# Attention scores contracted over 128 rows instead of twice 64, with q transposed by DMA in later pairs

## The chip, the cores and the metric

The kernel runs on one core of a Trainium2 chip. The metric is device time in microseconds, from the start to the end of one execution. Engines are named as in the profile: PE (TensorE, matmuls; its weight loads are PEld), DVE (VectorE), ACT (ScalarE), POOL (GpSimd), SP (SyncE, which here only issues DMAs).

## The reference

Two stages, with batch 4, 8 heads, 768 positions, head size 64.

The first is attention that chooses chunks. Keys are cut into 24 chunks of 32. For each query and chunk an upper bound of the score is computed from the chunk's elementwise minimum and maximum; causally later chunks get −1e9; the six chunks with the highest bounds are kept:

```python
k_min = np.min(k_chunks, axis=3); k_max = np.max(k_chunks, axis=3)
ub = np.sum(np.maximum(q * k_min, q * k_max), axis=-1)      # per query and chunk
ub = np.where(causal, ub, -1e9)
top_chunks = np.argsort(ub, axis=-1)[..., -6:]
scores = np.where(sel & causal_by_position, scale * (q @ k.T), -1e9)
attn = softmax(scores); x = attn @ v
```

The second is a gated MLP on `x` (heads side by side, 512 wide): `h = relu(x @ w_in)` with 1024 columns, halves `u` and `v`; `v` is normalised over its 512 columns, multiplied from the left by the 768×768 matrix `w_spatial`, a bias is added; the output is `(u * v_s) @ w_out`, in float32.

## The kernel before

Everything is cut into operations that a planner in the kernel (class `Plan`, L80) puts into one fixed order per engine before the program is written. Each operation has a list of engines that can do it with a cost for each, a priority (a due time), and the tiles that it reads and writes. The planner always takes one of the operations that can start soonest (within 60 ns) and of these the one with the lowest priority value, on the engine where it would end first. Tiles come from rings of a fixed number of buffers (L298 to L334). So a change of costs, ring sizes or operations shifts the order everywhere. On the chip every engine runs its list in order: an instruction that waits holds everything behind it on its engine, and the same goes for SP's list of DMAs.

The attention is done for 16 pairs of heads (4 batches of 4 pairs). Per pair `i`:

- `load` (L414): k, q and v of both heads by SP's DMAs, 384 KB each (L422).
- `prep` (L425): k and q are cast to float16 on POOL (`n16`, through the helper `copy`, L287 to L291). q is transposed by PE in all pairs, k by PE in pairs 0 to 3 (L442, six 128×128 transposes into PSUM), evacuated to `qT` and `kT` by ACT or DVE. In pairs 4 to 15 k is transposed by a DMA through the crossbar (L450) straight into `kT`. In the transposed tiles rows 0 to 63 are head 0 and rows 64 to 127 head 1. From `kT` DVE takes the chunk maxima and minima (`kh_half` L468 halves the chunk, `kmm` L471 reduces; from PSUM in one step, L460, in pair 0), from `qT` the positive and the negative part (`rq`, L481). PE multiplies them to bounds `ub` (L489); DVE adds the causal mask (L496), takes the eight largest of each row (L502, L507), and writes to `sn` what is not selected and a guard (L510, L513). PE transposes `sn` (L522), ACT or DVE evacuates it to `selT` (L525).
- `attend` (L530): scores of both heads, masked by adding a second product: `expand`, a constant pattern that spreads 24 chunks to 768 columns with −30000, times `selT`. For each strip of a key tile by up to 512 queries there are four matmuls of 64 rows: head 0 and head 1 of k·q (L546), then head 0 and head 1 of pattern·selection (L549), which are added in PSUM. Rows 0 to 63 and 64 to 127 hold the two heads. Six groups of strips per pair fill PSUM tiles `sc` (two buffers of 128×1024). ACT takes the exponential (L556), POOL zeroes the upper triangles (L566), PE multiplies with v (`av`, L578; a column of ones gives the sum), DVE takes reciprocals (L581) and normalises into `x16` (L584). `x16` is transposed by PE in pairs 0 to 7 and 15 (L597), otherwise by the crossbar (L603).

`mlp` (L608) runs once per batch when its four pairs are done: projections of v and u (L621), relu (L628 on ACT, L630 on DVE), statistics (L639, L642), normalisation (L654, DVE), the spatial product (L669), gating (L673), a transpose of the gated tile (L683 on PE in batches 0 and 3, else crossbar L689), the output projection (L695), its evacuation and the store (L699). The planner fits this into the gaps of later pairs' attention; the last batch has no attention beside it. `w_spatial` is transposed on PE at the beginning (L407).

The costs that the planner used for PE's scores include an entry for a switch of the row mode, `SWITCH = 60.0` ns a group (L551); a DMA costs a length and a common 1900 ns until it has landed.

Of the kernel before, what the change touches and what calls it, by code (L numbers as in the profile page):

```python
# [14 lines left out]
P = 128  # L15
# [7 lines left out]
LAT = {"PE": 210.0, "DVE": 130.0, "ACT": 140.0, "POOL": 160.0, "DMA": 1900.0}  # L23
# [6 lines left out]
def t_act(n):  # L30
    return n / 1.2 + 70.0
# [33 lines left out]
class Op:  # L65
    def __init__(self, name, opts, fn, prio):
        self.name, self.opts, self.fn, self.prio = name, opts, fn, prio
        self.preds, self.succs, self.bufs = set(), [], []
        self.opens = []
        self.dma = 0.0  # L70
        self.lazy = False
        self.start = self.end = self.ready = None
        self.eng = None
# [6 lines left out]
class Plan:  # L80
# [11 lines left out]
    def op(self, name, opts, fn, prio, reads=(), writes=(), dma=0.0, after=None, lazy=False):  # L92
# [32 lines left out]
    def run(self, window=60.0):  # L125
# [11 lines left out]
        while avail:  # L137
# [35 lines left out]
            if o.dma:  # L173
                dma_free = max(dma_free, s + d) + o.dma
                o.end = dma_free + LAT["DMA"]
            else:
                o.end = s + d
# [27 lines left out]
    def report(self, total):  # L205
# [4 lines left out]
        print("DMA", round(sum(o.dma for o in self.done)))  # L210
# [3 lines left out]
XBAR = 1200.0  # L214
PE_T = {("q", i) for i in range(16)} | {("k", i) for i in range(4)}
SWITCH = 60.0
# [7 lines left out]
LOAD = 1750.0  # L224
BACKLOG = 4000.0

STRIPS = [
    [(0, 0, 512, 0)],  # L230
    [(1, 128, 512, 0)],
    [(2, 256, 512, 0)],
    [(3, 384, 256, 0), (5, 640, 128, 256), (3, 640, 128, 384)],
    [(0, 512, 256, 0), (4, 512, 256, 256)],
    [(1, 640, 128, 0)],
]
WIDTHS = [512, 512, 512, 512, 512, 128]
DIAG = [(0, 2), (0, 2), (0, 2), (0, 4), (256, 2), None]
BANK = 512
EW = 2 * sum(WIDTHS)  # L240


def block_column(t, qi):
    for g, strips in enumerate(STRIPS):
        for (tt, q0, n, col) in strips:
            if tt == t and q0 <= qi * P < q0 + n:
                return g, col + qi * P - q0
    raise KeyError((t, qi))
# [3 lines left out]
def kernel(  # L252
# [49 lines left out]
    ring("kT", 4, [P, NQT, P])  # L302
    ring("qT", 4, [P, NQT, P])
    ring("selT", 3, [P, S])
# [7 lines left out]
    ring("e", 3, [P, EW])  # L312
# [20 lines left out]
    ring("ex24", 1, [P, 2, NCH], F32)  # L333
    ring("expand", 1, [P, S])  # L334
# [23 lines left out]
    ex24, expand = buf("ex24"), buf("expand")  # L358

    def mk_ex(e):  # L360
        for hi in range(2):
            x = ex24.t[:, hi, :]
            e.memset(x, 0.0)
            e.affine_select(out=x, in_=x, compare_op=Alu.not_equal, fill=NEG,
                            base=-hi * D, channel_multiplier=1, pattern=[[-1, NCH]])
            e.affine_select(out=x, in_=x, compare_op=Alu.not_equal, fill=-1.0,
                            base=-(hi * D + NCH), channel_multiplier=1, pattern=[[0, NCH]])
    preset("ex24", {"POOL": 1400.0}, mk_ex, [ex24], prio=-60.0)
    for hi in range(2):
        r0, r1 = hi * D, (hi + 1) * D  # L370
        preset(f"expand{hi}", {"ACT": 720.0},
               lambda e, hi=hi, r0=r0, r1=r1: copy(
                   e, expand.t[r0:r1].rearrange("p (c j) -> p c j", j=CHUNK),
                   ex24.t[r0:r1, hi].unsqueeze(2).to_broadcast([r1 - r0, NCH, CHUNK])),
               [(expand, hi)], reads=[ex24], prio=-50.0)
# [6 lines left out]

    preset_pool("vt", 80.0, lambda e, t: e.memset(t[:, :, :, D:D + 2], 1.0), -80.0)
# [4 lines left out]
    CAST0 = {"DVE": t_dve(S, 2)}  # L388
# [4 lines left out]
    def weights():  # L393
        for n, dst, src, cost in (("w_in", w_in, moe_w_in.rearrange("(o p) f -> p o f", p=P), 6200.0),
# [3 lines left out]
               0.0, writes=[dst], dma=cost, after=W_AFTER[n], lazy=True)  # L398
        op("bcol", {"SP": 350.0}, lambda e: e.dma_start(out=bcol.t, in_=moe_b_spatial.rearrange("(t p) -> p t", p=P)),
           30.0, writes=[bcol], dma=1200.0)  # L400
# [24 lines left out]
    def prep(i, prio):  # L425
# [3 lines left out]
        for n in ("k", "q"):  # L429
            nat = buf("n16")  # L430
            tT = st[n + "T"] = buf(n + "T")
# [3 lines left out]
            op(f"c_{n}{i}", CAST0 if i == 0 else CAST, go, prio, reads=[st[n]], writes=[nat])  # L435
            if (n, i) in PE_T:
                tr = buf("gen")

                def go(e, nat=nat, tr=tr):
# [4 lines left out]
                op(f"e_{n}{i}", {"ACT": t_act(S)} if i == 0 else EVAC,  # L444
                   lambda e, tr=tr, tT=tT: copy(e, tT.t.rearrange("p t c -> p (t c)"), tr.t.bitcast(F16)[:, 0:S]),
                   prio + 0.05, reads=[tr], writes=[tT])
                src[n] = (tr, lambda tr=tr: tr.t.bitcast(F16)[:, 0:S])
            else:
                def go(e, nat=nat, tT=tT):
                    e.dma_start_transpose(out=tT.t, in_=nat.t.rearrange("p t h d -> p (t h d)"))  # L450
                op(f"x_{n}{i}", {"SP": 1250.0}, go, prio, reads=[nat], writes=[tT], dma=XBAR)
            if i > 0 or (n, i) not in PE_T:
                src[n] = (tT, lambda tT=tT: tT.t.rearrange("p t c -> p (t c)"))
        kb, kT = src["k"]
        qb, qT = src["q"]
        kmm, km = buf("kmm"), buf("km")
        if kb.pool.name == "gen":
            for m, f in ((0, Alu.max), (1, Alu.min)):
                op(f"kmm{m}_{i}", {"DVE": t_dve(S)},
                   lambda e, m=m, f=f: e.tensor_reduce(kmm.t[:, m, :], kT().rearrange("d (c j) -> d c j", j=CHUNK),  # L460
                                                       axis=AX.X, op=f),
                   prio, reads=[kb], writes=[(kmm, m)])
        else:
            hf = buf("kh_half")
            for m, f in ((0, Alu.max), (1, Alu.min)):
                def go(e, m=m, f=f):
                    x = kT().rearrange("d (c j) -> d c j", j=CHUNK)
                    e.tensor_tensor(hf.t[:, m], in0=x[:, :, 0:CHUNK // 2], in1=x[:, :, CHUNK // 2:CHUNK], op=f)  # L468
                op(f"kh{m}_{i}", {"DVE": t_dve(S // 2, 2)}, go, prio, reads=[kb], writes=[(hf, m)])
                op(f"kmm{m}_{i}", {"DVE": t_dve(S // 2)},  # L470
                   lambda e, m=m, f=f: e.tensor_reduce(kmm.t[:, m, :], hf.t[:, m], axis=AX.X, op=f),  # L471
                   prio, reads=[(hf, m)], writes=[(kmm, m)])
        for hi in range(2):
            r0, r1 = hi * D, (hi + 1) * D
            op(f"km{hi}_{i}", {"POOL": 250.0, "DVE": 100.0} if i else {"DVE": 100.0},
               lambda e, hi=hi, r0=r0, r1=r1: copy(e, km.t[r0:r1, :, hi, :], kmm.t[r0:r1]), prio,
               reads=[kmm], writes=[(km, hi)])
        rq = buf("rq")
        for m, f in ((0, Alu.max), (1, Alu.min)):
            op(f"rq{m}_{i}", {"DVE": t_dve(S, 2 if qb.pool.name == "gen" else 4)},  # L480
               lambda e, m=m, f=f: e.tensor_scalar(rq.t[:, m, :], in0=qT(), scalar1=0.0, scalar2=None, op0=f),  # L481
               prio, reads=[qb], writes=[(rq, m)])
# [41 lines left out]
        selT = st["selT"] = buf("selT")  # L524
        op(f"es{i}", EVAC, lambda e: copy(e, selT.t, tr.t.bitcast(F16)[:, 0:S]), prio, reads=[tr], writes=[selT])  # L525
# [4 lines left out]
    def attend(i, prio):  # L530
        b, hp = divmod(i, HP)
        st = pair.pop(i)
        kT, qT, selT, vt = st["kT"], st["qT"], st["selT"], st["vt"]
        x16, e_ = buf("x16"), buf("e")
        for g, strips in enumerate(STRIPS):
            sc = buf("sc")
            w = WIDTHS[g]

            def go(e, strips=strips, sc=sc):
                for (t, q0, n, col) in strips:  # L540
                    for half in range(2):
                        for hi in range(2):
                            r = slice(hi * D, (hi + 1) * D)
                            o = sc.t[:, hi * BANK + col:hi * BANK + col + n]
                            if half == 0:
                                e.matmul(o, lhsT=kT.t[r, t, :], rhs=qT.t[r].rearrange("p t c -> p (t c)")[:, q0:q0 + n],  # L546
                                         start=True, stop=False)
                            else:
                                e.matmul(o, lhsT=expand.t[r, t * P:(t + 1) * P], rhs=selT.t[r, q0:q0 + n],  # L549
                                         start=False, stop=True)  # L550
            op(f"sc{i}_{g}", {"PE": t_pe(*[2 * s[2] for s in strips]) + SWITCH}, go, prio,  # L551
               reads=[kT, qT, selT, expand], writes=[sc])

            def go(e, g=g, w=w, sc=sc):
                o = e_.t[:, 2 * BANK * g:2 * BANK * g + 2 * w].rearrange("p (h c) -> p h c", h=2)
                e.activation(out=o, in_=sc.t.rearrange("p (h c) -> p h c", h=2)[:, :, 0:w],  # L556
                             func=Act.Exp, scale=scale)
# [193 lines left out]
```

## Time and profile before

| | us |
|---|---|
| median of three runs | 229.11 |
| lowest, highest | 228.91, 230.06 |
| the profiled execution | 229.7 |
| its span, from the first to the last instruction | 228.0 |

| engine | busy us of the span | instructions |
|---|---|---|
| PE | 198.6 (87%) | 2226 |
| DVE | 171.9 (75%) | 564 |
| ACT | 136.2 (60%) | 195 |
| POOL | 81.1 (36%) | 157 |

The profile comes from one execution. A group of instructions is given by line, engine, operation and `out<-in` of the tiles, with count, busy time and mean length; the idle time of the engine just before the group and what ended it stand behind. PE's matmuls overlap, so a matmul's length is more than what it costs; the distance between the starts of two that follow each other without a gap is the cost. The same holds to a smaller degree on DVE and ACT. "Issue" of a DMA is SP's time; "landing" is when the data are there.

### The profile page before, as it was taken

How to read it: one execution, taken by the hardware profiler on the slowest of the kernel's cores; microseconds unless marked ns; L12 is line 12 of the kernel's file. 1: busy time of each engine (PE TensorE's matmuls, PEld its weight loads, DVE VectorE, ACT ScalarE, POOL GpSimd, SP SyncE). 2: the span in 40 equal slices, each digit the busy share in tenths (PEclk: the TensorE clock that was granted, in tenths of full speed). 3: DMA queues.
4: the chain of work that ended last, by engine and by line, in shares of the span. 5: the costliest groups of instructions: out<-in, count | busy, mean ns of one | idle time of the engine just before them, and what ended most of it. 6: DMA issues, size and time to landing. Idle time of an engine off the chain costs nothing.

```text
span 228.0 us, 5782 instructions
## 1 busy us (share of the span) xinstructions
PE 198.6 (87%) x2226; PEld 111.2 (49%) x2226; DVE 171.9 (75%) x564; ACT 136.2 (60%) x195; POOL 81.1 (36%) x157
## 2 busy tenths in 40 slices
PE   1167778879959699998999999999999999999982
PEld 0144546564625365656464646455535644444440
DVE  3686999686998899989987999969536955383430
ACT  5208577729726985639657793718688540775062
POOL 3226774343910674737363464322232100000000
PEclk9999999999979999999999999999999999999998
DMA  8999998999999769999999993223541004630024
GB/s 156 201 218 218 180 185 138 209 221 192 209 169 220 130 138 167 223 214 201 184 226 243 176 179 63 57 50 90 163 144 35 3 0 92 203 121 3 0 94 182
DMA packets 102331, 33.60 MB, mean 147 GB/s; under 512 B 97440, under 2 KB 98720, under 8 KB 102304
## 3 DMA queue, kind: packets, MB, share of 16 engines
q1 hardware_dynamic: 100464, 30.49, 71.9%
q0 software_dynamic: 1840, 2.75, 7.2%
q8 instruction: 17, 0.28, 0.5%
q14 instruction: 10, 0.08, 0.1%
HBM read 24.38 MB, written 6.29 MB: 135 GB/s over the span
## 4 chain that ended last, share of the span: by engine, by line
PE 62%; DVE 28%; ACT 4%; issue 2%; DMA 2%; DVEq 0%; ACTq 0%
PE gen L621 16%; PE gen L669 13%; PE gen L695 8%; PE sc L546 6%; PE gen L578 5%; PE sc L549 5%; DVE rq L481 3%; DVE max L507 3%; DVE vn L654 3%; DVE x L584 3%; DVE kmm L471 2%; PE gen L442 2%; ACT e L556 2%; DVE kh_half L468 2%; PE gen L489 2%
## 5 line engine op out<-in xcount | busy, mean ns | idle before, releaser
L556 ACT ACTIVATE e<-sc 128x1024 f16<-128x1024 f32 (+1 forms) x96 | 84.2, 918 | 41.0 <-PE sc L549 40.2
L566 POOL TENSOR_SCALAR_AFFINE_SELECT e<-e 128x256 f16<-128x256 f16 (+1 forms) x80 | 37.2, 466 | 78.8 <-ACT e L556 78.6
L621 PE MATMUL gen<-w_in,xT 128*128 128x512 f16 x192 | 46.5, 385 | 0.2
L546 PE MATMUL sc<-qT,kT 64*128 64x128 f16 (+2 forms) x288 | 39.1, 295 | 2.5 <-ACT e L556 2.0
L549 PE MATMUL sc<-selT,expand 64*128 64x128 f16 (+2 forms) x288 | 38.0, 291 | 2.7 <-DVE selT L291 2.7
L669 PE MATMUL gen<-vn,wsT 128*128 128x512 f16 x144 | 33.1, 379 | 0.0
L621 PEld LDWEIGHTS <-xT 128*128 128x128 f16 x192 | 17.6, 99 | 22.1 <-issue 4.3
L673 DVE SCALAR_TENSOR_TENSOR g<-gen,bcol,u 128x512 f16<-128x512 f32 x24 | 17.8, 746 | 12.7 <-PE gen L669 10.5
L695 PE MATMUL gen<-w_out,gT 128*128 128x512 f16 x96 | 23.6, 380 | 1.3 <-DVE gT L291 0.6
L546 PEld LDWEIGHTS <-kT 64*128 64x128 f16 x288 | 15.3, 94 | 18.8 <-issue 12.0
L578 PEld LDWEIGHTS <-e 128*128 128x128 f16 x672 | 21.9, 97 | 4.8 <-issue 1.7
L578 PE MATMUL gen<-vt,e 128*128 128x65 f16 x672 | 23.1, 193 | 0.8 <-POOL e L566 0.8
L669 PEld LDWEIGHTS <-wsT 128*128 128x128 f16 x144 | 13.4, 98 | 16.3 <-issue 1.3
L639 DVE BATCH_NORM_STATS2 stats<-vraw 128x6 f32<-128x512 f32 x24 | 16.1, 681 | 7.0 <-ACT vraw L628 6.7
L289 ACT ACTIVATE o<-gen 128x512 f32<-128x512 f32 x22 | 13.1, 597 | 12.9 <-PE gen L695 12.8
L628 ACT ACTIVATE u<-gen 128x512 f16<-128x512 f32 x22 | 13.1, 597 | 12.2 <-PE gen L621 12.2
L442 PE MATMUL gen<-ident,n 128*128 128x128 f16 x120 | 11.3, 237 | 7.4 <-DVE n L291 7.4
L549 PEld LDWEIGHTS <-expand 64*128 64x128 f16 x288 | 14.7, 95 | 5.1 <-issue 3.1
L584 DVE TENSOR_TENSOR x<-gen,rec 128x384 f16<-128x384 f32 x32 | 16.9, 545 | 0.4
L654 DVE TENSOR_SCALAR vn<-vraw,mv,rstd 128x512 f16<-128x512 f32 x24 | 15.4, 686 | 1.4 <-ACT rstd L649 1.2
L291 POOL CAST vt<-vst 128x768 f16<-128x768 f32 x16 | 13.5, 844 | 7.2 <-DMA vst<-in_v_dram 6.1
L471 DVE TENSOR_REDUCE kmm<-kh_half 128x24 f16<-128x384 f16 x30 | 15.4, 538 | 0.0
(67 smaller groups left out, 238.9 us busy)
## 6 DMA issues: line engine op xcount, KB each, us to landing
kst<-in_k_dram SPq DMA_DIRECT2D x16, 384.0 KB, 6.4
qst<-in_q_dram SPq DMA_DIRECT2D x16, 384.0 KB, 6.3
vst<-in_v_dram SPq DMA_DIRECT2D x16, 384.0 KB, 5.8
out_dram<-o SPq DMA_DIRECT2D x24, 256.0 KB, 2.2
ws_raw<-in_moe_w_spatial_dram POOLq DMA_DIRECT2D x1, 1152.0 KB, 11.8
w_in<-in_moe_w_in_dram POOLq DMA_DIRECT2D x1, 1024.0 KB, 9.4
w_out<-in_moe_w_out_dram POOLq DMA_DIRECT2D x1, 512.0 KB, 7.8
kT<-n SPq DMA_TRANSPOSE x12, 4.2
```

The lines of the kernel that those rows point to most:

```text
L471: lambda e, m=m, f=f: e.tensor_reduce(kmm.t[:, m, :], hf.t[:, m], axis=AX.X, op=f),
L546: e.matmul(o, lhsT=kT.t[r, t, :], rhs=qT.t[r].rearrange("p t c -> p (t c)")[:, q0:q0 + n], start=True, stop=False)
L549: e.matmul(o, lhsT=expand.t[r, t * P:(t + 1) * P], rhs=selT.t[r, q0:q0 + n], start=False, stop=True)
L556: e.activation(out=o, in_=sc.t.rearrange("p (h c) -> p h c", h=2)[:, :, 0:w], func=Act.Exp, scale=scale)
L566: e.affine_select(out=d, in_=d, compare_op=Alu.is_ge, fill=0.0, base=0, channel_multiplier=-1, pattern=[[0, n], [1, P]])
L578: e.matmul(avv()[:, qi, :], lhsT=e_.t[:, c:c + P], rhs=vt.t[:, t, hi, 0:D + 1], start=(t == 0), stop=(t == qi))
L584: lambda e, rec=rec, avv=avv, hi=hi: e.tensor_tensor(x16.t[:, :, hi, :], in0=avv()[:, :, 0:D], in1=rec.t.to_broadcast([P, NQT, D]), op=Alu ...
L621: e.matmul(acc.t, lhsT=x.t[:, ko, t * P:(t + 1) * P], rhs=w_in.t[:, ko, c0:c0 + DH], start=(ko == 0), stop=(ko == NDO - 1))
L654: lambda e, h=h, r2=r2, t2=t2: e.tensor_scalar(vn[t2].t, in0=vraw[t2].t, scalar1=mv[h].t[:, r2, 0:1], scalar2=rstd[h].t[:, r2, :], op0=Alu ...
L669: e.matmul(acc.t, lhsT=wsT.t[:, s, t * P:(t + 1) * P], rhs=vn[s].t, start=(s == 0), stop=(s == NQT - 1))
L673: lambda e, t=t, acc=acc, g=g: e.scalar_tensor_tensor(g.t, in0=acc.t, scalar=bcol.t[:, t:t + 1], in1=u[t].t, op0=Alu.add, op1=Alu.mult),
L695: e.matmul(acc.t, lhsT=gT.t[:, ko, :], rhs=w_out.t[:, ko, :], start=(ko == 0), stop=(ko == KO - 1))
```

## The change

- The score's two products become one. For each head there are tiles `kh0`, `kh1` (768 columns, 128 rows): one half of the rows holds that head's k, the other half the constant pattern, which is written once into each of three buffers by ACT. Tiles `a0`, `a1` hold that head's q in the same half and the selection in the other. A strip takes one matmul of 128 rows per head.
- k and q get from the transposed tile (PSUM or SBUF) into these tiles by copies of 64 rows each: four per pair for k and q, from PSUM on ACT or DVE, from SBUF on DVE or POOL. The selection is evacuated by two copies of 64 rows.
- The scores are grouped by head, three groups each of 1024, 896 and 768 columns, with one mask on POOL per group; `e` holds one head, four buffers instead of three.
- q is transposed by the crossbar in pairs 4 to 15, as k is; PE transposes both in pairs 0 to 3. Their tiles `kT`, `qT` have three buffers instead of four and are written by the crossbar alone. In pairs 0 to 3 everything reads PSUM.
- `rq` may run on ACT too; its second half is now the negative part with its sign turned, and the minima are negated.
- The planner's costs: no `SWITCH`, 60 ns more for DVE operations on SBUF (`SHARED`), a DMA as a triple of issue, length and landing, and SP's list held back when the ring is full.

```diff
-PE_T = {("q", i) for i in range(16)} | {("k", i) for i in range(4)}
-SWITCH = 60.0
+PE_T = {(n, i) for n in "kq" for i in range(4)}
...
+SHARED = 60.0
+GROUPS = [
+    [(0, 0, 512, 0), (1, 128, 512, 512)],
+    [(2, 256, 512, 0), (3, 384, 384, 512)],
+    [(5, 640, 128, 0), (4, 512, 256, 128), (1, 640, 128, 384), (0, 512, 256, 512)],
+]
+WIDTHS = [1024, 896, 768]
...
-    ring("kT", 4, [P, NQT, P])
-    ring("qT", 4, [P, NQT, P])
-    ring("selT", 3, [P, S])
+    ring("kT", 3, [P, NQT, P])
+    ring("qT", 3, [P, NQT, P])
+    ring("kh0", 3, [P, S])
+    ring("kh1", 3, [P, S])
+    ring("a0", 3, [P, S])
+    ring("a1", 3, [P, S])
...
-    ring("e", 3, [P, EW])
+    ring("e", 4, [P, EW])
...
+    SPLIT = {"DVE": t_dve(S, 4) + SHARED, "POOL": t_pool(S)}
...
-                op(f"e_{n}{i}", {"ACT": t_act(S)} if i == 0 else EVAC,
-                   lambda e, tr=tr, tT=tT: copy(e, tT.t.rearrange("p t c -> p (t c)"), tr.t.bitcast(F16)[:, 0:S]),
-                   prio + 0.05, reads=[tr], writes=[tT])
...
+        for n, (sb_, sT), dst in (("k", src["k"], kh), ("q", src["q"], a)):
+            for hi in range(2):
+                r0, r1 = hi * D, (hi + 1) * D
+                ps_src = sb_.pool.name == "gen"
+                op(f"s{n}{hi}_{i}", {"ACT": t_act(S), "DVE": t_dve(S, 2)} if ps_src else SPLIT,
+                   lambda e, hi=hi, r0=r0, r1=r1, sT=sT, dst=dst: copy(e, dst[hi].t[r0:r1, :], sT()[r0:r1, :]),
+                   prio + 0.2, reads=[sb_], writes=[(dst[hi], "d")])
...
-        op(f"es{i}", EVAC, lambda e: copy(e, selT.t, tr.t.bitcast(F16)[:, 0:S]), prio, reads=[tr], writes=[selT])
+        for hi in range(2):
+            r0, r1 = (1 - hi) * D, (2 - hi) * D
+            op(f"es{hi}_{i}", EVAC,
+               lambda e, hi=hi, r0=r0, r1=r1: copy(e, a[hi].t[r0:r1, :], tr.t.bitcast(F16)[r0:r1, 0:S]),
+               prio + 0.2 * hi, reads=[tr], writes=[(a[hi], "s")])
...
+            for g, strips in enumerate(GROUPS):
+                sc = buf("sc")
...
+                    for (t, q0, n, col) in strips:
+                        e.matmul(sc.t[:, col:col + n], lhsT=kh[hi].t[:, t * P:(t + 1) * P],
+                                 rhs=a[hi].t[:, q0:q0 + n], start=True, stop=True)
```

In the order of the built program this gives: on PE 256 score matmuls for 576 and 48 transposes of k and q for 120; on DVE 407 entries for 386, on ACT 229 for 196, on POOL 20 copies of 64 rows more, on SP 12 more crossbar transposes (`qT<-n`).

## The prediction

> **What bounds the kernel now.** I read the busy times by stretch first, because the share over the whole span mixes stages with different limits. Columns: stretch and its length; busy us (x instructions) of PE, PEld, DVE, ACT, POOL; granted clock; DMA share; GB/s.
>
> ```profile
> 0.00:80.00 80.00, 56.70 (x754) 35.12 (x755) 63.86 (x226) 48.55 (x65) 36.82 (x74) 0.98 1.13 188
> 80.00:160.00 80.00, 78.67 (x1010) 45.54 (x1008) 74.01 (x268) 51.80 (x71) 38.98 (x73) 1.00 0.90 159
> 160.00:228.00 68.00, 63.18 (x474) 30.56 (x468) 33.99 (x72) 35.81 (x61) 5.26 (x12) 0.99 0.28 86
> ```
>
> ```profile
> 0.00:161.00 161.00, 136.37 (x1764) 80.98 (x1764) 138.71 (x495) 101.19 (x136) 75.91 (x146) 0.99 1.01 173
> ```
>
> Up to 80 us nothing is full; from 80 to 160 PE (98%) and DVE (93%) both are; from 160 on only PE is. The last selection, pair 15 (L513 on DVE, its transpose L522 on PE), ends on DVE at 160.8 us and starts on PE at 161.3, which is why the last row is cut there: behind it DVE has slack.
>
> Second, PE's timeline inside the full stretch (start us, duration us, instruction).
>
> ```profile
> 119.53 0.50 PE L442 MATMUL gen<-ident,n 128*128 128x128 f16 x6
> 119.96 0.39 PE L546 MATMUL sc<-qT,kT 64*128 64x512 f16 x2
> 120.18 0.38 PE L549 MATMUL sc<-selT,expand 64*128 64x512 f16 x2
> 120.40 0.38 PE L546 MATMUL sc<-qT,kT 64*128 64x512 f16 x2
> 120.61 0.38 PE L549 MATMUL sc<-selT,expand 64*128 64x512 f16 x2
> 120.93 1.04 PE L621 MATMUL gen<-w_in,xT 128*128 128x512 f16 x4
> 121.80 0.46 PE L489 MATMUL gen<-km,rq 128*128 128x48 f16 x12
> ```
>
> Durations overlap, so the cost is the distance between starts. Two 64-row matmuls of 512 columns, one per head, take 0.22 us together. The edges cost extra: six transposes take 0.43 when scores follow them and 0.335 elsewhere, the last score pair before L621 takes 0.32, not 0.22. Each unbroken run of score matmuls thus costs 0.1 us in front and 0.1 behind. PE's order has 61 such runs: 12.2 us. By starts, PE's 228.0 us are 5.0 before its first matmul, 175.8 of work, 12.2 at these edges, 31.7 idle (29.4 of it before 161.3) and 3.2 behind the last one.
>
> Third, DVE's groups up to 161 us (after the bar: busy us, mean ns; then idle before).
>
> ```profile
> L481 DVE TENSOR_SCALAR rq<-qT 128x768 f16<-128x768 f16 x30 | 13.1, 469 | 0.3
> L468 DVE TENSOR_TENSOR kh_half<-kT 128x384 f16<-128x384 f16 x30 | 12.6, 440 | 0.0
> L654 DVE TENSOR_SCALAR vn<-vraw,mv,rstd 128x512 f16<-128x512 f32 x12 | 9.6, 830 | 0.3 <-ACT rstd L649 0.2
> ...
> L291 DVE COPY selT<-gen 128x768 f16<-128x768 f16 x13 | 7.1, 544 | 0.8 <-PE gen L522 0.7
> ```
>
> The SBUF-only groups (rq, kh_half, vn, km, the small L510) have long means: rq takes 0.35 us where no POOL instruction overlaps it and up to 0.97 where one does; selT, which reads PSUM, stays at 0.54 either way. Over the unhindered value these groups lose 13.1 us on 107 instructions, 0.12 each, with POOL busy 75.9 of 161 us (47%).
>
> **The change, part by part.**
>
> *PE.* Score columns stay the same: 5376 per pair, then one head's k·q and its selection pattern in one 128-row matmul instead of two heads' halves side by side. A 128-row matmul of 512 columns costs 0.216 by starts (L621: four in 0.865), so a pair's scores cost 2.27 us for 2.33: −1.0 in all. All 61 runs lose their edges: −12.2, as nothing of 64 rows is left on PE. Pairs 4 to 15 lose q's transposes, 12 × 0.335: −4.0. New PE work is 175.8 − 5.0 = 170.8 with no edges, 17.2 us less. A fork: if the 0.1 us belonged to the score matmuls and not to their row count, 12.2 of it would stay; no other change of kind on PE shows it (av to proj, transposes to spatial: 0), so I take zero, keeping 12.2 as the other end.
>
> The Trainium skill, "TensorEngine Tiling (Array Packing)", section "Theoretical Speedup", speaks against the change: operands of up to 64 rows gain up to 2× by row tiling, so giving it up would double the score stream, an estimate of 36 us more. The rows above say that it isn't given up for nothing: two products are stacked in one contraction. No run here shows the doubled stream.
>
> *DVE up to the last selection*, counted in the order of both programs, at costs by starts. Gone: 15 evacuations of k and q at 0.46, three of w_spatial at 0.46, one q cast at 0.47, six kh_half at 0.27 and six halved reductions at 0.46, 16 rq (SBUF) at 0.27 (13 rq go to ACT), one relu 0.6: −18.1. New: nine half copies from PSUM and three more of the selection at 0.46, 28 half copies from SBUF at 0.27 (64 rows cost what 128 do, since columns count; bounded by rq's 0.27 and kh_half's 0.27 from below and by the 0.46 of a PSUM copy), six full reductions from PSUM at 0.88, three rq at 0.48, four km at 0.09, and 13 that now stand ahead of this point (two evacuations each of o, xT and gT, two normalisations, three reciprocals, one statistics with its aggregate): 4.7. In sum +24.9. Net +6.8. If the 28 copies cost 0.46, 5.3 more.
>
> *The port wait.* POOL gets 20 of the split copies (0.77 each by starts, as its casts of 768 columns): +15.4, and 96 triangle masks of 256 elements for 64 of 256 and 16 of 512: +1.8; some 92 us busy, 57%. Ten more DVE instructions are of the hindered sort: 117 × 0.12 × 57/47 = 17.0, for 13.1: +3.9. From below 0; from above twice that.
>
> The Trainium skill, "SBUF — State Buffer", section "SBUF: two separate sides", makes this an exclusive lock: the later instruction blocks for the whole of the earlier. Half a POOL instruction (0.4) at a share of 57% for 117 instructions is an estimate of 27 us, 14 more than now; the measured 0.12 is below what it would make, and the forecast stays with the measured value.
>
> *When the last selection ends.* DVE busy: 138.7 + 6.8 + 3.9 = 149.4. Its idle time before 161 us is 22.3: 4.4 until the first load, 17.9 later, of which 12 were ended by PE. With PE going from 98% to some 85% of the stretch I let two thirds of those 12 go (nearest row: 80 to 160, where PE is full and DVE idles 6.0), leaving 9.9. 149.4 + 4.4 + 9.9 = 163.7 us, against 160.8 now. Both ends: none left, 153.8; all left, 171.7.
>
> *From there to the end* PE is the bound. Now: from 161.3, the transpose 0.34, work 59.3, 15 edges 1.5, idle 2.3, last stores 3.2: 228.0. After: the order puts one more o, one more v, five score groups' and three av's worth ahead of it, so 53.4 of work and no edges: 0.34 + 53.4 + 2.3 + 3.2 = 59.2. The scores' groups wait for ACT's exps there; ACT is 52% busy from 161 on, so they don't set the pace.
>
> *Hidden at nothing.* ACT gains some 24 us (22 half copies for 7 evacuations and 13 rq, 0.7 each by starts, six presets at 0.74 for two, one cast of q; the exps cover the same columns in as many instructions): 101.2 + 24 = 125 of 164, 76%. DVE's 91% covers it. If it doesn't, PE waits for exps, 0.92 each. The six presets (4.4 from about 2.1) and the cast end before 8.2, where q's first transposes start now.
>
> *The sum.* 163.7 + 0.5 + 59.2 = 223.4 us of span, 4.6 less. The profiled execution took 229.7 for its span of 228.0, so 225.1; it lies 0.6 above the median of the runs, 229.1, so **224.5**.
>
> **Rivals.**
>
> *PE alone sets the pace.* If DVE keeps up, the last selection waits only for PE: work 117.4 up to it (116.5 plus 10.6 of edges now), 5.0 and the same 29.4 idle: 151.8, then 59.2: 211.0, a time of 212. For it: PE's idle in the first 80 us comes from chains that get shorter, k's reductions and q's rq read PSUM without a copy between. Against: DVE needs 149.4 + 4.4 = 153.8 with no gap at all.
>
> *DVE's idle time isn't PE's.* All 17.9 stays: 171.7 + 0.5 + 59.2 = 231.4, a time of 232.5. For it: 16.1 of the 22.3 lies before 80 us, where PE isn't full. Against: the rows name PE as releaser.
>
> *Late crossbars (slower).* Now DVE never waits for kT.
>
> ```profile
> kT<-n SPq DMA_TRANSPOSE x12, 4.2
> ```
>
> In pairs 4 to 15 q too goes cast (POOL), crossbar (SP), then split copies and rq. Two transposes of 1.2 us issue stand in SP's queue, where loads stand behind them, and those behind POOL's masks; landing took 2.7 to 6.3 us here. kT and qT have three buffers, not four. DMA moves some 0.9 us more per pair in a stretch where its share is already 0.90. If q lands late, the DVE instruction at the head of its queue holds masks' maxima, selections and normalisations of other pairs. At 1 us per pair, 12 us: 163.7 + 12 + 0.5 + 59.2 = 235.4, a time of 236.5. It decides from 4.6/12 = 0.4 us per pair, where the gain is gone. Against: casts stood 10 us ahead of kh_half in the middle pairs (pair 9: crossbar issued 85.7, used 96).
>
> **Numbers.** Forecast 0.50, PE's pace 0.10, idle stays 0.20, crossbars 0.20. Differences under 0.5% (228.0 to 230.3) are about what a measurement tells from none. Nearly all of the first and all of the second are faster: 0.59; the edges of the others 0.11 the same; 0.30 slower. Range 213 to 235: from DVE without gaps, less a little, to the crossbar case.
>
> **What would show it.** Right: no 0.1 us edges around the scores; PE's sum of work near 171; DVE's busy time before the last selection near 149 and that selection ending near 164; some 59 us from there to the end. Wrong: DVE or POOL waiting for qT<-n or kT<-n; rq and split copies on DVE over 0.5 us in the mean; PE waiting for ACT's exps in total over 5 us.

## The result and the profile after

The changed kernel takes 242.69 us (median of four runs, 240.22 to 243.24) against 229.59 for the kernel before (four runs, 228.91 to 230.14): 1.0551 times as long, 95% interval 1.047 to 1.0633. The forecast was 224.5, faster, with a range of 213 to 235; the kernel became slower instead, and the time lies above the range. The profiled execution took 242.4 for a span of 240.6, which is 12.6 more span than before. DVE has 574 instructions in the profile for 564, 10 more and not the 21 of the list before the prediction; ACT has 227 for 195. Ratios below leave out slow runs, those over 1.5% above the fastest of the same kernel (two of four of `no_split_sel_one`, one each of `split_by_dma` and `before_q_xbar_costs`), and the profiles of the first two are of such runs and 1 to 2% long.

The busy times by stretch, cut where the last selection's transpose starts on PE, now 181.1. Columns as in the prediction: stretch and length, busy us (x instructions) of PE, PEld, DVE, ACT, POOL, then granted clock, DMA share, GB/s.

```profile
0.00:80.00 80.00, 53.95 (x574) 34.86 (x574) 58.82 (x201) 59.64 (x79) 39.40 (x79) 0.96 1.08 178
80.00:161.00 81.00, 68.41 (x730) 40.29 (x730) 75.10 (x249) 54.20 (x76) 47.06 (x83) 0.98 0.89 167
...
0.00:181.10 181.10, 138.96 (x1499) 85.29 (x1500) 151.37 (x514) 129.67 (x174) 98.23 (x182) 0.96 0.95 169
181.10:240.60 59.50, 54.40 (x336) 26.72 (x334) 29.66 (x61) 30.31 (x54) 3.50 (x8) 1.00 0.31 90
```

In the middle stretch PE fell from 98% to 84% and DVE stayed at 93%. The last selection comes 19.8 us later (161.3 to 181.1); behind it the kernel is 7.2 us shorter (66.7 to 59.5). DVE's two parts up to the cut: busy 151.4 for 138.7, idle 29.7 for 22.6.

PE's timeline, at the place that answers to the one shown of before:

```profile
120.69 0.80 PE L586 MATMUL gen<-vt,e 128*128 128x65 f16 x21
121.32 0.54 PE L566 MATMUL sc<-a,kh 128*128 128x512 f16 x2
121.70 1.02 PE L629 MATMUL gen<-w_in,xT 128*128 128x512 f16 x4
```

A score group of 512 + 384 columns takes 0.38 from its first start to that of the next group (121.32 to 121.70), which is 896 columns at the 0.216 us per 512 of other 128-row matmuls. The 0.1 us at the edges is gone, in front and behind.

DVE's groups up to 181 us (busy us, mean ns; idle before):

```profile
L481 DVE TENSOR_TENSOR kh_half<-kT 128x384 f16<-128x384 f16 x24 | 12.1, 528 | 0.1
...
L293 DVE COPY km<-kmm 64x48 f16<-64x48 f16 x23 | 7.8, 338 | 0.3
...
L293 DVE COPY kh<-kT 64x768 f16<-64x768 f16 x14 | 7.1, 509 | 0.0
L293 DVE COPY a<-qT 64x768 f16<-64x768 f16 x14 | 7.1, 505 | 0.2
...
L498 DVE TENSOR_SCALAR rq<-qT 128x768 f16<-128x768 f16 x11 | 5.3, 480 | 0.0
```

The 28 new half copies from SBUF cost 14.2 us of DVE, and `kh_half`, which nobody changed, went from 440 to 528 ns in the mean.

The waits of the whole span (who waits for whom: us in total, times, longest):

```profile
ACT a L291 <- DVE a L293: 16.0, 8, 6.2
...
PE sc L566 <- ACT e L570: 6.0, 12, 1.0
...
DVE a L293 <- ACT a L291: 4.9, 8, 1.3
...
POOL a L293 <- DMA qT<-n: 2.4, 2, 1.6
```

The first and the third row are new: an operation that writes `a` waits for another that writes `a`. The second is one of the prediction's signs of being wrong (PE waiting for exponentials over 5 us in total). The last row is all that an engine waits for the crossbar's q directly.

### The profile page after: what moved, and what is told of

It is laid out like the page before. It is cut to its first block, busy times and chain, and to the rows that moved or that the text cites. A ratio compares the mean times of both kernels' runs of the same rounds, so it can differ in the third digit from the quotient of the medians.

```text
span 240.6 us, 5117 instructions
## 1 busy us (share of the span) xinstructions
PE 193.4 (80%) x1834; PEld 112.0 (47%) x1834; DVE 181.0 (75%) x574; ACT 160.0 (66%) x227; POOL 101.7 (42%) x189
## 4 chain that ended last, share of the span: by engine, by line
DVE 40%; PE 39%; ACT 9%; issue 6%; POOL 3%; DMA 2%; ACTq 0%; DVEq 0%; POOLq 0%
PE gen L629 10%; PE gen L677 8%; DVE a L293 6%; PE gen L703 6%; PE sc L566 5%; ACT e L570 5%; DVE kmm L484 4%; PE gen L586 3%; DVE kh_half L481 3%; DVE x L592 3%; DVE max L527 3%; DVE rq L498 3%; DVE km L293 3%; DVE g L681 2%; ACT a L291 2%
## 5 line engine op out<-in xcount | busy, mean ns | idle before, releaser
L570 ACT ACTIVATE e<-sc 128x768 f16<-128x768 f32 (+2 forms) x96 | 84.1, 914 | 19.3 <-PE sc L566 17.1
L577 POOL TENSOR_SCALAR_AFFINE_SELECT e<-e 128x256 f16<-128x256 f16 x96 | 41.3, 433 | 68.9 <-ACT e L570 68.1
L566 PE MATMUL sc<-a,kh 128*128 128x512 f16 (+3 forms) x256 | 52.0, 325 | 9.9 <-ACT e L570 6.0
L566 PEld LDWEIGHTS <-kh 128*128 128x128 f16 x256 | 21.7, 101 | 22.9 <-issue 15.1
L586 PE MATMUL gen<-vt,e 128*128 128x65 f16 x672 | 26.7, 196 | 4.6 <-POOL e L577 4.0
L291 ACT ACTIVATE a<-gen 64x768 f16<-64x768 f16 x17 | 13.7, 804 | 19.2 <-DVE a L293 16.0
L509 PE MATMUL gen<-km,rq 128*128 128x48 f16 x192 | 8.6, 191 | 12.2 <-DVE km L293 8.3
L293 DVE COPY a<-gen 64x768 f16<-64x768 f16 x23 | 12.8, 556 | 6.1 <-ACT a L291 4.9
L509 PEld LDWEIGHTS <-rq 128*128 128x128 f16 x192 | 7.3, 101 | 18.2 <-DVE km L293 6.8
L293 POOL CAST n<-qst 128x768 f16<-128x768 f32 x15 | 13.6, 905 | 3.1 <-DMA qst<-in_q_dram 2.9
```

The costliest lines, as they stand in the source:

```text
L291: e.activation(out=out, in_=in_, func=Act.Copy)
L293: e.tensor_copy(out, in_)
L566: e.matmul(sc.t[:, col:col + n], lhsT=kh[hi].t[:, t * P:(t + 1) * P], rhs=a[hi].t[:, q0:q0 + n], start=True, stop=True)
L570: lambda e, g=g, sc=sc, e_=e_: e.activation(out=e_.t[:, BASES[g]:BASES[g] + WIDTHS[g]], in_=sc.t[:, 0:WIDTHS[g]], func=Act.Exp, scale=scale),
L577: e.affine_select(out=d, in_=d, compare_op=Alu.is_ge, fill=0.0, base=0, channel_multiplier=-1, pattern=[[0, 2], [1, P]])
L586: e.matmul(avv()[:, qi, :], lhsT=e_.t[:, c:c + P], rhs=vt.t[:, t, hi, 0:D + 1], start=(t == 0), stop=(t == qi))
```

## The experiments

In the expectations, theory A puts the loss on the half copies from SBUF (their time on DVE and the wait between DVE and POOL), theory B on half copies of one PSUM tile by two engines that follow each other, theory C on late crossbars; theory D, in a later round, says that DVE's idle time isn't made by PE.

All profiles are in one table. "Cut" is when the last selection's transpose starts on PE; DVE's busy time is up to there, idle is the cut less that, and the rest is the span less the cut. The time is the median of all runs of a kernel; the other columns are of the one profiled execution.

| kernel | time | cut | DVE busy | DVE idle | rest |
|---|---|---|---|---|---|
| before | 229.6 | 161.3 | 138.7 | 22.6 | 66.7 |
| after | 242.7 | 181.1 | 151.4 | 29.7 | 59.5 |
| q_on_pe | 250.9 | 186.5 | 159.0 | 27.5 | 62.5 |
| no_split | 227.7 | 167.4 | 137.2 | 30.2 | 59.4 |
| pool_split_short | 236.7 | 175.3 | 145.7 | 29.6 | 59.5 |
| sel_one_engine | 235.7 | 175.9 | 157.9 | 18.0 | 57.3 |
| planner_bank | 236.6 | 174.9 | 156.6 | 18.3 | 59.3 |
| no_split_sel_one | 223.1 | 166.5 | 143.9 | 22.6 | 57.4 |
| split_by_dma | 238.6 | 186.4 | 151.6 | 34.8 | 53.4 |
| after_pe_light | 229.1 | 180.9 | 152.4 | 28.5 | 47.5 |
| before_pe_light | 217.2 | 160.0 | 140.6 | 19.4 | 55.3 |
| before_q_xbar | 223.6 | 171.2 | 141.5 | 29.7 | 50.6 |
| before_q_xbar_costs | 225.1 | 161.4 | 134.7 | 26.7 | 59.5 |
| before_q_xbar_pairs | 234.0 | 171.5 | 146.3 | 25.2 | 61.1 |

### Is it the crossbar? q back on PE, and q's crossbar alone

Label `q_on_pe`, an edit of the changed kernel:

```diff
-PE_T = {(n, i) for n in "kq" for i in range(4)}
+PE_T = {("q", i) for i in range(16)} | {("k", i) for i in range(4)}
```

> The changed kernel with q transposed on PE in all pairs again (k as in the change); q's halves, rq and sign part then read PSUM. Theory A (DVE's work and its waits for the port shared with POOL, from 72 us on, set the pace): 24 half copies go from SBUF to PSUM at 0.46 for 0.27 to 0.5, PE gets 4 us more; 238 to 245, no gain. Theory B (readers of one PSUM tile on two engines must follow each other, so ACT and DVE stand at the head of their queues): more such readers, 243 to 250. Theory C (q lands late from the crossbar): 228 to 234, and the waits of DVE and POOL for qT are gone.

Measured: 250.89, 1.0905 times before (1.0867 to 1.0943). Slower still, and above the ranges of all three theories. Theory C is out: q through PSUM, with two half copies of one tile in every pair, costs more than the crossbar. By the table it is DVE's work that grew (busy 159.0 for 151.4), not its idle time (27.5 for 29.7), so theory B's reason for its range isn't what is seen.

Label `before_q_xbar`, an edit of the kernel before:

```diff
-PE_T = {("q", i) for i in range(16)} | {("k", i) for i in range(4)}
+PE_T = {(n, i) for n in "kq" for i in range(4)}
```

> The kernel before with only q's crossbar in pairs 4 to 15 added. Theories A and B: PE loses 12 x 0.335 = 4.0 us of transposes and DVE and ACT 12 evacuations of 0.46 to 0.7, nothing is added: 222 to 227. Theory C: DVE waits for qT at the head of its queue in twelve pairs: 232 to 240.

Measured: 223.59, 0.9707 times before (0.969 to 0.9725): this line alone, without the rest of the change, is the fastest version found here that leaves nothing out. The waits of the changed kernel agree that the crossbar harms nobody: 2.4 us of POOL's, none of DVE's, with a landing of `qT<-n` of 2.9 us in the median (2.7 to 12.6).

### The half copies from SBUF

Label `no_split` keeps the program and its order, but each half copy from SBUF carries 8 columns, so most of k and q is left out:

```diff
-lambda e, hi=hi, r0=r0, r1=r1, sT=sT, dst=dst: copy(e, dst[hi].t[r0:r1, :], sT()[r0:r1, :]),
+lambda e, r0=r0, r1=r1, sT=sT, d=dst[hi], w=S if ps_src else 8: copy(e, d.t[r0:r1, 0:w], sT()[r0:r1, 0:w]),
```

> The changed kernel in the same order, but the 48 half copies of k and q from SBUF (pairs 4 to 15) copy 8 columns, not 768, so most of the k and q that the later scores use are old ones. Theory A: DVE loses 28 x 0.27 to 0.5 and most of the port waits (POOL loses 20 x 0.77): 14 to 18 us less, 225 to 229. Theory B: 236 to 241. Theory C: no change, 240 to 243.

Measured: 227.67, 0.9885 times before (0.9847 to 0.9922), 15.0 less than the change as it is. DVE's groups up to 167.4 us say where it went, by the same rows as above:

```profile
L481 DVE TENSOR_TENSOR kh_half<-kT 128x384 f16<-128x384 f16 x24 | 8.3, 368 | 0.1
...
L293 DVE COPY km<-kmm 64x48 f16<-64x48 f16 x23 | 5.7, 246 | 0.3
...
L498 DVE TENSOR_SCALAR rq<-qT 128x768 f16<-128x768 f16 x11 | 3.9, 358 | 0.0
...
L293 DVE COPY a<-qT 64x8 f16<-64x8 f16 x14 | 3.5, 252 | 0.2
...
L293 DVE COPY kh<-kT 64x8 f16<-64x8 f16 x14 | 3.2, 229 | 0.0
```

The copies themselves are 7.5 us shorter (14.2 to 6.7). Three groups whose instructions are the same (`kh_half`, `km`, `rq`) are 7.3 us shorter. The sum, 14.8, is about the 14.2 by which DVE's busy time fell and the 13.7 by which the cut came earlier. DVE's idle time hardly moved (29.7 to 30.2). In this order a microsecond less of DVE's work up to the cut is about a microsecond less of time. This is theory A. The 28 copies of 8 columns still take DVE 6.7 us, so the 15.0 is the price of their columns, not of all that the copies cost.

Label `pool_split_short` shortens only POOL's 20 copies (those leave out their columns):

```diff
-copy(e, dst[hi].t[r0:r1, :], sT()[r0:r1, :])
+copy(e, dst[hi].t[r0:r1, 0:8 if e is nc.gpsimd else S], sT()[r0:r1, 0:8 if e is nc.gpsimd else S])
```

> The changed kernel in the same order, but the 20 half copies that POOL has copy 8 columns; DVE's 28 stay (some k and q in later pairs are old). Theory A1 (it is POOL's hold on the port that costs): of the 15.0 us of no_split 8 to 12 come back here, 231 to 235. Theory A2 (it is DVE's own time for its 28 copies): 2 to 4 us, 239 to 241.

Measured: 236.66, 1.0275 times before (1.023 to 1.0319), 6.0 less, between the two expectations. DVE's busy time up to the cut fell 5.7 with not one DVE instruction changed. The rows that answer to those above:

```profile
L481 DVE TENSOR_TENSOR kh_half<-kT 128x384 f16<-128x384 f16 x24 | 9.0, 396 | 0.1
L293 DVE COPY km<-kmm 64x48 f16<-64x48 f16 x23 | 8.3, 363 | 0.3
L293 DVE COPY a<-qT 64x768 f16<-64x768 f16 x14 | 6.1, 436 | 0.2
L293 DVE COPY kh<-kT 64x768 f16<-64x768 f16 x14 | 5.3, 381 | 0.0
L498 DVE TENSOR_SCALAR rq<-qT 128x768 f16<-128x768 f16 x11 | 4.8, 440 | 0.0
```

DVE's own half copies are 2.8 us shorter (14.2 to 11.4), and the three other groups 2.5 (25.2 to 22.7), a third of the 7.3 above; `km` is no shorter at all. So of the 15.0 about 6 come with POOL's 20 copies, by way of the DVE instructions that read SBUF beside them. About 9 go only when DVE's own 28 copies are short too: 4.7 of that is these copies' own time, and why the other groups become shorter with them isn't shown.

### The two copies of the selection

In pair 8 of the changed kernel, the two copies from one PSUM tile, first on DVE's timeline, then on ACT's:

```profile
111.08 0.56 DVE L293 COPY a<-gen 64x768 f16<-64x768 f16 x1
```

```profile
111.67 0.80 ACT L291 ACTIVATE a<-gen 64x768 f16<-64x768 f16 x1 [1.27 <-DVE a L293]
```

ACT's starts 0.03 us after DVE's has ended, and ACT had stood idle for 1.27 us. In none of the 16 pairs do the two overlap, in 15 they are on two engines. The program makes an engine that reads a PSUM tile wait for another engine's read of the same tile, though here the rows differ (0 to 63 and 64 to 127). The planner had counted the two as parallel, so ACT's queue, with its exponentials, stands until DVE has made its copy.

Not all of the 16.0 us is this wait, though. The longest of them, with the transposes that both copies need and DVE's copy:

```profile
87.51 0.50 PE L542 MATMUL gen<-ident,sn 128*128 128x128 f16 x6
```

```profile
88.24 0.56 DVE L293 COPY a<-gen 64x768 f16<-64x768 f16 x1
```

```profile
88.84 0.80 ACT L291 ACTIVATE a<-gen 64x768 f16<-64x768 f16 x1 [6.15 <-DVE a L293]
```

The transposes end at 88.01, so of these 6.15 us at most 0.83 are due to DVE; the rest is a copy that stands at the head of ACT's queue before its data are there. Counted so from each trace row, 7.3 of ACT's 16.0 us and 4.5 of DVE's 4.9 come after both the transposes and the engine were ready.

The Trainium skill, "PSUM — Partial Sum Buffer", section "PSUM bank collisions raise a hardware error", wants different engines kept apart in one bank only where they touch the same quadrant of 32 partitions; by it the two copies might run side by side. No run here tried that.

Label `sel_one_engine` makes both copies one operation of the planner, on one engine:

```diff
-        for hi in range(2):
-            r0, r1 = (1 - hi) * D, (2 - hi) * D
-            op(f"es{hi}_{i}", EVAC, ...)
+        def go(e):
+            for hi in range(2):
+                r0, r1 = (1 - hi) * D, (2 - hi) * D
+                copy(e, a[hi].t[r0:r1, :], tr.t.bitcast(F16)[r0:r1, 0:S])
+        op(f"es{i}", {"ACT": 2 * t_act(S), "DVE": 2 * t_dve(S, 2)}, go, prio, reads=[tr],
+           writes=[(a[0], "s"), (a[1], "s")])
```

> The changed kernel with both half copies of a pair's selection from PSUM made one operation on one engine, so that neither ACT nor DVE waits for the other's half; the planner's order shifts. Theory A: DVE's work is the same, 239 to 244. Theory B: the 16 us that ACT waits for DVE at these copies and DVE's 4.9 for ACT go: 229 to 236. Theory C: 240 to 244.

Measured: 235.65, 1.0239 times before (1.0193 to 1.0284), 7.0 less than the change. Of its waits, this is the row that was 16.0:

```profile
ACT a L291 <- DVE a L293: 1.1, 1, 1.1
```

DVE is 6.5 us busier up to the cut, since it now has more of these copies, and its idle time is 11.7 lower: 29.7 to 18.0. A good part of that is time in which DVE stood for the product with v, here before, in the changed kernel and in this run:

```profile
DVE rec L581 <- PE gen L578: 3.9, 3, 2.2
```

```profile
DVE rec L589 <- PE gen L586: 9.9, 8, 2.6
```

```profile
DVE rec L590 <- PE gen L587: 4.8, 4, 2.4
```

Label `planner_bank` leaves the operations as they are and only lets the planner know of the wait:

```diff
+                    held = [t + LAT[e2] for b in o.bufs if b.pool.name == "gen"
+                            for e2, t in b.last.items() if e2 != e]
-                    best.append((max(r, free[e]), o.prio, e, d, o))
+                    best.append((max([r, free[e]] + held), o.prio, e, d, o))
```

> The changed kernel, where the planner alone is changed: it knows that an operation on another engine that reads the same PSUM tile can't start before the one before it has ended. Same instructions, other order and engines. Theory B as a matter of order: most of what sel_one_engine gained, 233 to 238. Rival: the order was as good as it gets, the serial copies themselves cost: 240 to 245.

Measured: 236.64, 1.0271 times before (1.0231 to 1.0311), 6.1 less; no wait of ACT for DVE at `a` is left, and DVE's idle time is 18.3. The long wait of ACT is still there, in the same pair and now named after its transposes:

```profile
ACT a L296 <- PE gen L547: 5.9, 1, 5.9
```

The planner puts both copies of the selection on DVE in 12 pairs, on ACT in one, on two engines in three. Two different edits agree on 6 to 7 us, as theory B said. But both also take copies off ACT (busy up to the cut 124.3 and 121.0, for 129.7) and change the order of everything, so how much of the gain is the wait itself isn't shown.

Label `no_split_sel_one`: both (k and q left out as in `no_split`).

> Both of the above: the selection's half copies as one operation on one engine, and the SBUF half copies of k and q cut to 8 columns (old k and q are used in later pairs). no_split gave 227.7, sel_one_engine 235.7, from 242.7. If A (DVE's work and port waits) and B (engines that wait for each other at one PSUM tile) are two separate costs, they add up: 242.7 - 15.0 - 7.0 = 220.7, so 218 to 223. If they are one cost seen twice, 226 to 229.

Measured: 0.9608 times before (0.955 to 0.9665), by two runs of 220.92 and 221.77; the median of all four is 223.05, at the upper edge of the first range. 242.7 − 15.0 − 7.0 = 220.7: the two costs add, within a microsecond or two. What `sel_one_engine` changes is not the cost of the half copies under another name.

Label `split_by_dma`: the half copies from SBUF as DMAs of SP, on top of `sel_one_engine`:

```diff
+                if not ps_src:
+                    op(f"s{n}{hi}_{i}", {"SP": 600.0}, ... e.dma_start(out=dst[hi].t[r0:r1, :], in_=sT()[r0:r1, :]),
+                       prio + 0.2, reads=[sb_], writes=[(dst[hi], "d")], dma=(650.0, 500.0, 900.0))
+                    continue
```

> The selection's copies on one engine, and the 48 half copies from SBUF made by DMAs on SP (64 rows of 1536 bytes each) instead of DVE and POOL; the order shifts. Theory A plus B: as good as leaving them out if DMA has room, 219 to 226. Rival: SP's queue and the DMA engines (loads, 24 crossbars and 48 copies) become the bound, DVE waits for what lands late: 232 to 245.

Measured: 238.62, 1.0321 times before (1.0249 to 1.0393): no gain over 235.65, in the rival's range. In the profile, of its longest run (241.53), DVE is 6.2 us less busy than in `sel_one_engine`, but idles 34.8 us for 18.0. The work went off DVE and came back as idle time; what DVE waits for isn't settled, since the order moved as well.

### Does PE set DVE's pace?

Labels `after_pe_light` and `before_pe_light`: the projections use two of four matmuls and the spatial product three of six (the other half of both contractions is left out). That takes 84 matmuls of 512 columns (0.216 us each by starts, 18 us of PE) out from ahead of the last selection, and as many from behind it:

```diff
-                for ko in range(NDO):
+                for ko in range(2):
...
-                for s in range(NQT):
+                for s in range(3):
```

> The changed kernel in the same order, with half of the matmuls of both projections and of the spatial product left out (2 of 4 and 3 of 6; the MLP's result is another): 18.6 us of PE's work less before the last selection, some 18 behind it. Theory D (DVE's idle time does not come from PE's load): the last selection stays within 5 us of 181, total 219 to 225. Theory E (the step of the prediction: a lighter PE frees DVE): it falls by 10 or more, total 205 to 214.

> The same left out of the kernel before, in its own order. There PE is 98% busy from 80 to 160. Theory D: the last selection stays near 161, total 210 to 213. Theory E: it falls by 6 to 11 us, as far as the 12 us that DVE waits for PE, total 200 to 206.

Measured: 229.12 for the changed kernel, 0.996 times before (0.9922 to 0.9998), and 217.19 for the other, 0.9428 (0.9407 to 0.9448). The stretches up to the last selection, of `before_pe_light` and then of `after_pe_light`:

```profile
0.00:160.00 160.00, 124.61 (x1684) 75.14 (x1684) 140.62 (x495) 100.59 (x137) 76.42 (x146) 0.97 1.00 174
```

```profile
0.00:180.90 180.90, 129.12 (x1414) 78.92 (x1414) 152.35 (x514) 128.75 (x174) 96.56 (x182) 0.92 0.96 166
```

18 us less of PE's work by starts moved the last selection by 1.3 us in the kernel before and by 0.2 in the changed one. PE's busy time up to there fell by less, 12.1 and 9.8 us, at a granted clock that also fell (0.99 to 0.97 and 0.96 to 0.92). DVE idles 19.4 for 22.6 and 28.5 for 29.7. Even the kernel before, with PE at 98% of the middle stretch, did not have PE as its pace there: with PE at 87% (69.9 of the 80 us) the cut hardly moved. What the lighter PE gained lies behind the last selection: 66.7 to 55.3 and 59.5 to 47.5. Theory D named this; both times are higher than its range, as the rest shrank by 11 to 12 us, not by the full 18 of PE's work there.

### The other parts

Label `before_q_xbar_costs`: `before_q_xbar` with the planner's part of the change (but `SWITCH` and the rings stay as before), that is the new costs, the triples for DMAs, SP's list held back, and `rq` also on ACT:

```diff
+SHARED = 60.0
...
+                free[e] = max(s + d, dma_free - RING) if e == "SP" else s + d
...
+            op(f"rq{m}_{i}", {"DVE": t_dve(S, 2) if qb.pool.name == "gen" else t_dve(S, 4) + SHARED, "ACT": t_act(S)},
```

> The kernel before with q's crossbar in pairs 4 to 15 and all of the change but its 128-row scores: the planner's new costs, the DMA model, rq on ACT too. If the new costs and rq on ACT are good in themselves: 218 to 223 (before_q_xbar gave 223.6). If the order they make is worse: 225 to 231.

Measured: 225.06, 222.63 to 226.96, 0.9734 times before (0.9665 to 0.9804). It can't be told from `before_q_xbar`, so in that kernel these parts gain 1 us at best and cost some 3 at worst (222.63 to 226.96 beside 223.6); they didn't make the loss of 13.

Label `before_q_xbar_pairs`: `before_q_xbar` with two score groups in a row, to have fewer edges (47 unbroken runs of scores for 60) without 128-row operands:

```diff
+            if g % 2 == 0:
+                two = [(g, buf("sc")), (g + 1, buf("sc"))]
...
+                       reads=[kT, qT, selT, expand], writes=[sc for _, sc in two])
```

> The kernel before with q's crossbar in pairs 4 to 15, and score groups issued two by two, so that there are fewer runs of 64-row matmuls and fewer 0.1 us edges. If the edges cost time on a full PE: 48 runs or fewer for some 57, 2 us or more less than 223.6, 219 to 222. Rival: PE waits until both score tiles are free and ACT idles in between: 226 to 236.

Measured: 233.96, 1.0157 times before (1.0113 to 1.0201), 10.4 more than with single groups. The wait of the exponentials for scores, of `before_q_xbar` and then of `before_q_xbar_pairs`:

```profile
ACT e L556 <- PE sc L549: 37.7, 33, 6.2
```

```profile
ACT e L562 <- PE sc L554: 61.8, 25, 6.9
```

13 edges fewer would be 13 × 0.2 = 2.6 us of PE. With both PSUM buffers held for one operation, ACT waits 24 us more, as the rival said. By the table the loss lies behind the cut, which did not move (171.2 and 171.5): the rest grew from 50.6 to 61.1 us, with 10.3 us more of PE's busy time left there. Making PE's pieces coarser was a bad trade here.

## Why the prediction was wrong

**PE's terms: right.** No edges, 48 transposes of k and q for 120, and a sum of work by starts of 170.8, as predicted. From the last selection to the end it took 59.5, predicted 59.2.

**DVE's instructions: right.** By the same costs as in the prediction the work up to the last selection grew by 7.4 (predicted 6.8), counted in the order of the built program. Busy time up to there is 151.4, predicted 149.4.

**The port wait: right in sum, in part by luck.** DVE's SBUF instructions lose 16.3 us over their unhindered values, predicted 17.0 (13.7 before, by the same measure). The prediction had called means above 0.5 us for `rq` and the split copies a sign of being wrong; the half copies are there (505 and 509 ns, `rq` at 480), and 14.0 of the 16.3 us gather behind 72 us. What it did not see is how the sum is composed: without the half copies' columns (`no_split`) the loss is 6.5, so these copies' columns make some 10 us of it, and the rest of the change had taken 7 away (13.7 to 6.5). The Trainium skill's exclusive lock ("SBUF — State Buffer", "SBUF: two separate sides") agrees with single losses on the half copies (the longest `a<-qT` takes 0.98 us, the shortest 0.343); the 27 us that the prediction had estimated from it is not what the trace shows. Nor does a DVE instruction always wait for one POOL instruction alone: the copy below, of a kind that takes 0.16 us at its shortest, lasted across four that began after it (`vt`, `e`, `n`, `e`, 92.35 to 94.66).

```profile
92.20 2.49 DVE L293 COPY km<-kmm 64x48 f16<-64x48 f16 x1
```

**The step that failed: DVE's idle time.** "With PE going from 98% to some 85% of the stretch I let two thirds of those 12 go […], leaving 9.9." With the start's 4.4 that made 14.3; measured are 29.7. Of the 15.4 between:

- 8.0 (22.3 by the prediction's count, less 14.3) is idle time that was to go and did not. It had been put down to PE because PE was named as the last releaser. The two runs with a light PE show that PE was only the last link: take 18 us of its work out, and DVE idles 1 to 3 us less.
- 7.4 is new, and the prediction had no term for it. The new waits in the trace are those of two engines that must read one PSUM tile one after the other, and stand in their queues meanwhile. `sel_one_engine` and `planner_bank` give 7.0 and 6.1 us of time back, though, as said above, their orders differ too.

The two figures are arithmetic, not two measurements: with these waits gone DVE's idle time is 18.0 and 18.3, less than the 22.6 before, while its busy time is 5 to 7 us higher than in the changed kernel.

In sum: 2.0 of busy time + 15.4 of idle + 0.3 behind, less the 0.5 of hand-over that the measured idle time includes, is 17.2, which is 240.6 − 223.4.

**The rivals.** "DVE's idle time isn't PE's" had the mechanism; its 232.5 lacks the new 7.4 us and the 2.0 of busy time. "PE alone sets the pace" is refuted by the light PE, "late crossbars" by 2.4 us of waits and by `before_q_xbar`.

**Where the gain went.** The change's PE saving is real, but up to the last selection PE merely stands longer: its idle time by starts grew from 29.5 to 58.9 us. It paid only behind the cut, 7.2 us, while DVE brought the cut 19.8 later. Part by part, from the medians: q by crossbar −6.0 to −6.8 (223.6 from 229.6, or from the 230.4 measured beside it); the half copies' columns +15.0, the selection on two engines +7.0; what is then left for 128-row scores is 242.7 − 223.6 − 22.0 = −2.9. These come from different rounds, which differ by up to 1 us in the kernel before, and from programs in different orders, so the figure is rough: some 3 us is what 13.2 us of PE work was worth, less what half copies of 8 columns and all else in the change still cost. Taken directly, `no_split_sel_one` (220.92 to 225.58) beside `before_q_xbar` (223.56 to 223.68) leaves it open whether there is any gain.

**What stays open.** Of what DVE's remaining 18 to 23 us of idle time are made (chains between several engines; their last link names no cause). How much is order: `before_q_xbar` is fastest with a late cut and 29.7 us of DVE's idle time, because its planner had put more of PE's work ahead of the cut (rest 50.6), so neither the cut nor the idle time alone ranks two kernels with different orders. How the 6 to 7 us of the selection divide between the wait, ACT's load and the order. And whether the two copies could share a PSUM tile safely by rows.

## What to carry to other kernels

A busy engine that is named as the last releaser isn't thereby the pace: before idle time of one engine is credited to work saved on another, take that work out and see whether the idle time moves. The same goes for a wait between two copies: look when the data that both need were ready. Here the operands assembled by copies were paid for on the engines that copy and by the instructions that ran beside the copies; count such a price against what the matmul saves in the stretch where the matmul engine really is the bound. Before a tile is read by two engines "in parallel", see whether the program lets them, and let the planner know.

## What the runs showed of the hardware

- A run of 64-row score matmuls between 128-row matmuls cost 0.1 us in front and 0.1 behind (0.43 for 0.335 and 0.32 for 0.22 in the kernel before); with 128-row scores there was no such cost (0.38 us for a group of 896 columns, with other 128-row matmuls next to it).
- A copy of 64 rows from SBUF took DVE what 128 rows take: the shortest `a<-qT` is 0.343 us, as the shortest `rq` of 128 rows; with 8 columns instead of 768 it still takes 0.23 to 0.25 in the mean.
- The mean granted clock was 0.989 in the kernel before, 0.972 in the changed one and 0.935 in the changed one with the light PE. It doesn't follow PE's busy share alone: 0.987 in `no_split` (busy 83% of the span) and 0.960 in `before_q_xbar_pairs` (84%). No run here tells why.
